# A two-dimensional spectral filter with FFN on one core: table loads, read back and the order of the spectral steps

## The chip, the cores and the metric

The kernel runs on one core of a Trainium2 chip. The metric is device time in microseconds for one execution of the whole program; the median of several runs counts. Engine names are those of the profile: PE (TensorE), PEld (its weight loads), DVE (VectorE), ACT (ScalarE), POOL (GpSimd), SP (SyncE).

## What is computed

The reference, cut to what matters, works on x of 2048 x 1024 in bf16:

```python
def A(x, w_r, w_i):                       # spectral filter
    X = rfft2(x.astype(f32))              # over both axes
    return irfft2(X * (w_r + 1j * w_i), s=(2048, 1024)).astype(bf16)
def B(x, w1, b1, w2):                     # FFN, 1024 -> 3584 -> 1024
    h = x @ w1 + b1
    return (h * tanh(softplus(h))) @ w2
x = x + A(layernorm(x)); x = x + B(layernorm(x))
x = x + A(layernorm(x)); x = x + B(layernorm(x))
```

So there are two spectral stages and two FFN stages, one after the other.

## The kernel before

The program is a list of instructions per engine (PE, DVE, ACT, POOL, SP) that a small planner in Python writes out. `Prog.add` puts down the waits: every tile has a `Res`, which knows its writers and readers, and each engine runs its list strictly in order. DMAs are issued from the lists of SP, POOL and ACT; an issue that has to wait stops everything behind it on that engine.

A spectral stage (`layer_A`) turns the two-dimensional transform into matmuls with tables. The 2048 rows are split into 16 x 128, the 1024 columns into 8 x 128. Stage 1 (`s1`, PE L635) transforms the short axes of both. Then the work is cut into eight groups, g = 0 to 7, of two slots each, and each group has four steps with two halves each:

- `s2(g, half)`, PE L741: the long column transform into Z. Half 0 is copied from PSUM by ACT (L776), half 1 by ACT or DVE (L776 or L778); the next step of either slot needs both halves.
- `s3(g, i)`, PE L786 to L789: the long row transform with the forward table FT, copied out by ACT (L793), then multiplied by the filter with four DVE instructions (L797 to L804), into YK.
- `i1(g, i)`, PE L815: the inverse row transform with the back table BT, copied into V by ACT (L826); group 7 is split between DVE and ACT (`copy`, L578 and L574).
- `i2(g, half)`, PE L840 and L872: the inverse column transform into U, copied by ACT (L884), or by DVE (L882) for (3, 1) and (5, 1); group 7 again split between both.

After the second half of `i2`, `u_turn` writes U to DRAM (`u_scratch`) and `u_back` reads an earlier group back with another layout into UT. Group 7 goes in two halves, both written from ACT's list, and `u_last` reads it in six parts, four from SP and two from ACT. When all of UT is there, the last short transform runs (`i4`, PE L1041). While PE waits for it, it runs `spin` (L652), `residual_first` (L1030) and `hold` (L657).

The order of the steps is written out by hand in `order_A`: "320" is step 3 (`s3`) of group 2, half 0; both spectral stages use the same list. Each step takes the next of four pairs of PSUM banks in turn (`pair`).

In the first spectral stage (li = 0) the filter of each group is made on the way: `filter_bins(g)` (PE L1002, two DVE copies L1013, two ACT copies L1017) follows s2(g, 1) for g = 0 and 1 and s2(g, 0) for the others; `load_w` brings its input over POOL's list, and `keep_filter` stores the result for the second stage, after s3(g, 1), from POOL's list too. In the second stage `load_w` reads the stored filter.

The tables FT and BT have rings of three slots. `open_tables` loads the first ones, from SP in the first stage and from POOL in the second (there already during the first FFN stage, since it is called from `layer_B`). The later ones are loaded from POOL, after s3(g, 1) for FT and i1(g, 1) for BT. All DMAs have line L251, that of the helper `dma`.

Of the kernel before, what the change touches and what calls it, by code (L numbers as in the profile page):

```python
# [180 lines left out]
class KB:  # L181
# [482 lines left out]
    def open_tables(self, li):  # L664

        self.li = li
        self.WT = self.ring("WT", 4 if li else 8, 2048, [2, 512])
        self.FTr = self.ring("FT", 3, 1536, [2, 384])
        self.BTr = self.ring("BT", 3, 1536, [2, 384])
        if li == 0:  # L670
            self.WR = self.ring("WR", 3, 4096, [2, 2, 512])
        for g in range(2):
            self.load_w(g)
        for g in range(2 + li):
            self.load_tabs(g, li == 0)
        for g in range(2):
            self.load_btabs(g, li == 0)

    def rest_of_filter(self):

        self.WT += [self.alloc(f"WT{i}", self.o["WT"] + 2048 * i, [2, 512]) for i in range(4, 8)]
        gate = Res("gate")
        for r in self.r_xr[1:3]:
            gate.inherit(r)
        for g in (2, 3):
            self.load_w(g, [gate])

    def load_tabs(self, g, sp=False):
        b = self.FTr[g % 3]
        self.dma(self.sp if sp else self.pool, b.ap, self.con["FT"][g], f"ft{g % 3}{sp}", writes=[b.res])  # L690

    def load_btabs(self, g, sp=False):
        b = self.BTr[g % 3]
        self.dma(self.sp if sp else self.pool, b.ap, self.con["BT"][g], f"bt{g % 3}{sp}", writes=[b.res])
# [9 lines left out]
    def load_w(self, g, after=()):  # L704
        if self.li == 0:
            self.load_wr(self.wr(g), g)
            return
        i = 2 * g % 8
        self.dma(self.pool, self.wt_pair(i), self.w_d[g], f"wt{g % 4}", reads=[self.r_wd[g]] + list(after), writes=[w.res for w in self.WT[i:i + 2]])

    def layer_A(self, li):
# [13 lines left out]
        def filter_bins(g):  # L725
            ps, banks, _ = self.pair()
            self.filter_bins(g, ps, banks, self.wr(g), WT[2 * g % 8:2 * g % 8 + 2], o["WT"] + 2048 * (2 * g % 8),
                             self.JT, self.r_jt, dve)

        def zslot(g, i):  # L730
            return Z[(2 * g + i) % 6]

        def s2(g, half):

            ps, banks, _ = self.pair()
            y = self.Y.ap
            at = lambda r: y[:, r * 8 + g, :]
            fns = []

            def mm(dst, r, t, n, start, stop):  # L740
                fns.append(lambda e: e.matmul(dst, at(r), FD[:, t:t + n], start=start, stop=stop))  # L741
            if half == 0:
                for i in range(2):
                    d = ps[:, i * 512:(i + 1) * 512].rearrange("p (r k) -> p r k", r=2)
                    for kd in range(2):
                        for c in range(2):
                            mm(d[:, :, kd * P:(kd + 1) * P], 4 * kd + 2 * c + i, kd * 512 + c * 256, 256, c == 0, c == 1)
            else:
                d3 = ps[:, 0:512].rearrange("p (s r k) -> p s r k", s=2, r=2)
                for i in range(2):  # L750
                    for c in range(2):
                        mm(d3[:, i, :, :], 8 + 4 * c + i, 1024 + c * 256, 256, c == 0, c == 1)

                dd = ps[:, 512:1024].rearrange("p (s r d k) -> p d s r k", s=2, r=2, d=2)
                for kd in range(2):
                    r, t = 10 + 4 * kd, (3 + kd) * 512
                    if g == 0:
                        for i in range(2):
                            mm(dd[:, kd, i, :, :], r + i, t, P, True, True)
                    else:  # L760
                        for c in range(2):
                            mm(dd[:, kd, :, :, :], r + c, t + c * 256, 256, c == 0, c == 1)
            self.group(fns, reads=[self.Y.res, self.r_fd], writes=banks)
            za, zb = zslot(g, 0), zslot(g, 1)

            zz = self.ARENA[:, o["Z"] // 2 + (2 * g % 6) * K:o["Z"] // 2 + (2 * g % 6 + 2) * K].rearrange(
                "p (s r k) -> p s r k", s=2, r=2)
            if half == 0:
                za.res.begin()
                zb.res.begin()  # L770
            dst, src = zz[:, :, :, 256 * half:256 * half + 256], ps.rearrange("p (s r k) -> p s r k", s=2, r=2)
            if half:
                dst = dst.rearrange("p s r (b k) -> p s r b k", b=2)
                src = ps.rearrange("p (b s r k) -> p s r b k", b=2, s=2, r=2)
            if half == 0 or g < 3:
                self.op(act, lambda e: e.activation(dst, src, ACT.Copy), reads=banks, parts=[za.res, zb.res])  # L776
            else:
                self.op(dve, lambda e: e.tensor_copy(dst, src), reads=banks, parts=[za.res, zb.res])  # L778
# [107 lines left out]
        def u_turn(g, half):  # L886

            u = U[g % 3]
            if g == 7:
                h = slice(8 * half, 8 * half + 8)  # L890
                if half == 0:
                    u_back(6)
                self.dma(act, self.u_d[g][:, h, :], u.ap[:, h, :], f"uwh{half}", reads=[u.res], writes=[self.r_ud7[half]])
                if half:
                    u_last()
            elif half:
                self.dma(sp, self.u_d[g], u.ap, f"uw{g % 3}", reads=[u.res], writes=[self.r_ud[g]])
                if g:
                    u_back(g - 1)

        def open_ut():
# [6 lines left out]
        def u_back(g):  # L908
            if self.UT is None:
                open_ut()  # L910
            self.dma(sp, self.UT.ap[g:P:8, :, :], self.u_d[g].rearrange("l r n -> r l n"), f"usp{g % 3}",
                     reads=[self.r_ud[g]], parts=self.r_ut)

        def u_last():

            def back(prog, half, q, n):
                l = slice(32 * q, 32 * q + 32 * n)
                self.dma(prog, self.UT.ap[7 + 64 * half:P if half else 64:8, l, :], self.u_d[7][l, 8 * half:8 * half + 8, :].rearrange("l r n -> r l n"),
                         f"ul{half}{q}", reads=[self.r_ud7[half]], parts=self.r_ut[q:q + n])
            back(sp, 0, 0, 2)  # L920
            back(sp, 0, 2, 2)
            for q in range(4):
                back((act, sp)[q % 2], 1, q, 1)
# [17 lines left out]
        for stage, g, h in self.order_A():  # L941
            if stage == 2:
                s2(g, h)
                if li == 0 and h == (g < 2):
                    filter_bins(g)
                    if g in (0, 1):
                        load_w(g + 5)
                    elif g == 4:
                        load_w(7)
            elif stage == 3:  # L950
                s3(g, h)
                if h:
                    if li <= g < 6:
                        load_tabs(g + 2)
                    if li == 0:
                        self.keep_filter(g)
                    elif g < 4:
                        load_w(g + 4)
            elif stage == 4:
                i1(g, h)  # L960
                if h and g < 6:
                    load_btabs(g + 2)
            else:
                i2(g, h)
                u_turn(g, h)
# [9 lines left out]
    @staticmethod  # L975
    def order_A():


        order = ("200 201 210 300 211 301 220 310 400 221 311 401 230 320 410 500 231 321 411 501 330 331 420 510 240 511 421 241 "
                 "250 251 340 341 520 350 430 260 521 431 440 261 351 441 530 531 360 361 450 451 540 541 550 270 551 271 460 461 "  # L980
                 "370 371 560 561 470 471 570 571")
        return [tuple(map(int, w)) for w in order.split()]

    def load_wr(self, wr, g):
# [798 lines left out]
```

## Time and profile before

| | |
|---|---|
| median of 6 runs | 930.54 us (927.76 to 933.35) |
| the profiled execution | 930.39 us, of it 928.5 us from the first to the last instruction (the span) |
| granted TensorE clock | 0.998 of full speed |
| PE busy | 879.3 us, 95% of the span |
| DVE, ACT, POOL busy | 67%, 47%, 17% |
| DMA | 175.99 MB, on average 190 GB/s |
| first spectral stage, groups | about 37 to 113 us |
| second spectral stage, groups | about 494 to 562 us |
| PE L1329 and L1230 (FFN) | 340.2 and 280.3 us busy |

How to read it: times on the timeline are microseconds from the start of the span. A line of the timeline has start, duration, engine, line of the kernel, operation and operands, the number of instructions merged into it, and in brackets the idle time of the engine before it with what ended that idle time. Ends of matmuls are modelled: on PE the distance from one start to the next says what a group of matmuls costs. The chain lists the work that ended last, followed back from the end, in order of time: start, duration, engine, line.

### The profile page before, as it was taken

The numbers are of one execution on the slowest core, as the hardware profiler recorded it, in microseconds if no ns is written. First come the engines' busy times: TensorE is split into PE (matmuls) and PEld (weight loads), VectorE is DVE, ScalarE is ACT, GpSimd is POOL, SyncE is SP. The second block draws the span as 40 slices with busy tenths as digits, with TensorE's granted clock in tenths as the row PEclk, the third lists the DMA queues.
The fourth block names the chain that finished last, engine by engine and source line by source line (L and its number), as shares of the span: only waits on it lengthen the run. The fifth ranks groups of instructions, "written<-read, shape, count | busy, mean of one in ns | idle before, by whom it ended". The sixth has DMA issues, their size and how long they took to land.

```text
span 928.5 us, 13616 instructions
## 1 busy us (share of the span) xinstructions
PE 879.3 (95%) x5503; PEld 471.2 (51%) x5503; DVE 620.2 (67%) x985; ACT 435.9 (47%) x645; POOL 159.0 (17%) x187
## 2 busy tenths in 40 slices
PE   0899889999999999999999988999999999999998
PEld 0667476444444444444456766754444444444443
DVE  7798368686789667568766755666747655554473
ACT  7998385456213485520019865757550015552000
POOL 5642003960004641010121200000000000000000
PEclk9999999999999999999999999999999999999999
DMA  9979762674786388364723894445156645832432
GB/s 295 286 226 280 205 187 63 222 277 123 277 258 244 141 314 295 127 228 143 283 91 114 227 223 129 152 159 169 50 191 192 194 134 193 277 120 84 172 121 111
DMA packets 145839, 175.99 MB, mean 190 GB/s; under 512 B 66904, under 2 KB 124344, under 8 KB 145656
## 3 DMA queue, kind: packets, MB, share of 16 engines
q1 hardware_dynamic: 132816, 128.29, 44.5%
q0 software_dynamic: 10864, 45.19, 13.6%
q10 hardware_dynamic: 2096, 1.64, 0.6%
q8 instruction: 43, 0.70, 0.3%
q14 instruction: 20, 0.16, 0.1%
HBM read 130.78 MB, written 40.89 MB: 185 GB/s over the span
## 4 chain that ended last, share of the span: by engine, by line
PE 86%; DMA 4%; DVE 4%; ACT 3%; SPq 2%; issue 1%; POOL 0%; ACTq 0%; DVEq 0%
PE PS L1329 35%; PE PS L1230 30%; PE PS L1190 6%; PE PS L741 3%; PE PS L815 3%; PE PS L840 2%; PE PS L1041 2%; SPq L251 2%; DMA ARENA<-in_A_x_dram 1%; DMA ARENA<-in_B_w_dram 1%; DMA u_scratch<-ARENA 1%; PE PS L1151 1%; DMA ARENA<-u_scratch 1%; ACT ARENA L452 1%; PE PS L786 1%; PE PS L652 1%
## 5 line engine op out<-in xcount | busy, mean ns | idle before, releaser
L1329 PE MATMUL PS<-ARENA 128*128 128x512 bf16 x1568 | 340.2, 379 | 0.2 <-DMA ARENA<-in_B_w_dram 0.2
L1230 PE MATMUL PS<-ARENA 128*128 128x512 bf16 (+1 forms) x1288 | 280.3, 379 | 0.8 <-DVE ARENA L1235 0.8
L1329 PEld LDWEIGHTS PS<-ARENA 128*128 128x128 bf16 x1568 | 153.3, 98 | 185.0 <-DVE ARENA L1372 0.7
L1235 DVE TENSOR_TENSOR ARENA<-PS,ARENA 128x512 f32<-128x512 f32 x230 | 157.0, 690 | 100.8 <-PE PS L1230 93.0
L1230 PEld LDWEIGHTS PS<-ARENA 128*128 128x128 bf16 x1288 | 125.4, 98 | 153.1 <-DVE ARENA L1235 3.5
L1240 ACT ACTIVATE ARENA<-ARENA,B 128x512 bf16<-128x512 f32 x138 | 98.8, 721 | 69.1 <-DVE ARENA L1235 63.8
L574 ACT ACTIVATE ARENA<-PS 128x512 f32<-128x512 f32 (+3 forms) x86 | 61.6, 726 | 113.9 <-PE PS L1230 92.9
L1123 POOL TENSOR_TENSOR ARENA<-ARENA 128x512 bf16<-128x512 bf16 x56 | 71.1, 1269 | 75.6 <-DVE ARENA L523 61.2
L452 ACT ACTIVATE ARENA<-XS 128x1024 bf16<-128x1024 bf16 x60 | 63.2, 1053 | 36.2 <-DVE XS L1380 33.0
L1190 PE MATMUL PS<-ARENA 128*128 128x256 bf16 (+1 forms) x528 | 75.0, 299 | 3.4 <-DVE ARENA L1156 1.9
L1354 DVE TENSOR_TENSOR ARENA<-ARENA 128x3584 bf16<-128x3584 bf16 x32 | 63.8, 2015 | 0.0
L1190 PEld LDWEIGHTS PS<-ARENA 128*128 128x128 bf16 x528 | 50.9, 99 | 23.0 <-DVE ARENA L1156 3.3
L1380 DVE TENSOR_TENSOR XS<-PS,ARENA 128x512 bf16<-128x512 f32 x52 | 35.7, 689 | 38.9 <-PE PS L1329 38.5
L1372 DVE TENSOR_TENSOR ARENA<-PS,ARENA 128x512 f32<-128x512 f32 x48 | 32.9, 687 | 28.0 <-PE PS L1329 27.6
L1194 ACT ACTIVATE ARENA<-PS,B 128x256 bf16<-128x256 f32 (+1 forms) x66 | 33.2, 515 | 30.3 <-PE PS L1190 30.0
L1240 ACT ACTIVATE ARENA<-PS,B 128x512 bf16<-128x512 f32 x46 | 31.5, 685 | 18.4 <-PE PS L1230 18.4
L1368 DVE TENSOR_TENSOR ARENA<-ARENA,XS 128x512 f32<-128x512 f32 x52 | 36.8, 731 | 0.6
L443 ACT ACTIVATE RS<-MV,EPS 128x1 f32<-128x1 f32 (+2 forms) x11 | 3.3, 296 | 71.7 <-DVE MV L565 70.1
L797 DVE TENSOR_TENSOR ARENA<-ARENA 128x1024 bf16<-128x1024 bf16 x32 | 22.0, 687 | 20.5 <-ACT ARENA L793 14.8
L815 PE MATMUL PS<-ARENA 128*128 128x256 bf16 x256 | 32.3, 273 | 3.3 <-DVE ARENA L804 3.2
L793 ACT ACTIVATE ARENA<-PS 128x1024 bf16<-128x1024 f32 x32 | 32.7, 1052 | 4.8 <-PE PS L789 4.8
L741 PE MATMUL PS<-FD,ARENA 128*128 128x256 bf16 (+1 forms) x256 | 31.8, 271 | 2.5 <-ACT ARENA L641 1.3
(100 smaller groups left out, 823.8 us busy)
## 6 DMA issues: line engine op xcount, KB each, us to landing
ARENA<-in_B_w_dram SPq DMA_DIRECT2D x30, 896.0 KB, 6.8
ARENA<-w1s_scratch SPq DMA_DIRECT2D x28, 896.0 KB, 4.7
ARENA<-w2s_scratch SPq DMA_DIRECT2D x24, 896.0 KB, 6.6
w1s_scratch<-ARENA POOLq DMA_DIRECT2D x14, 896.0 KB, 4.4
ARENA<-in_B_w_dram SPq DMA_DIRECT2D x24, 512.0 KB, 4.3
u_scratch<-ARENA SPq DMA_DIRECT2D x14, 512.0 KB, 3.9
ARENA<-u_scratch SPq DMA_DIRECT2D x14, 512.0 KB, 6.8
w2s_scratch<-ARENA POOLq DMA_DIRECT2D x8, 896.0 KB, 4.1
```

Source lines behind the costliest of these rows:

```text
L452: self.op(act, lambda e, i=i, f=f: e.activation(junk.ap, x, f, accum_out=sums[:, i:i + 1]), reads=[self.r_xs[j]], writes=[junk.res], parts ...
L574: fn = (lambda e: e.activation(dst, src, ACT.Copy)) if scale is None else \
L741: fns.append(lambda e: e.matmul(dst, at(r), FD[:, t:t + n], start=start, stop=stop))
L815: fns.append(lambda e, c=c, part=part: e.matmul(ps[:, c * 256:(c + 1) * 256], yk.ap[:, part, c * P:(c + 1) * P], t[:, (128, 0)[part]:(384, ...
L1123: self.op(self.pool, lambda e, dst=A(dst), x=A(x), y=A(y), op=op: e.tensor_tensor(dst, x, y, op), reads=[b.res] + list(after), writes=[b.rs])
L1190: fns.append(lambda e, db=db, bank=bank, fl=fl: e.matmul(PS[:, bank, 0:w], wb.ap[:, db, fl * P:(fl + 1) * P], x.ap[:, db, tok], start=(db ...
L1230: self.group([lambda e, db=db: e.matmul(PS[:, bank, :], A[:, db, :], mov[:, db, :], start=(start and db == 0), stop=(db == 3), skip_group_ ...
L1235: self.op(dve, lambda e: e.tensor_tensor(dst.ap, PS[:, bank, :], x.ap, ALU.add), reads=[self.r_bank[bank], x.res], writes=[dst.res])
L1240: self.op(act, lambda e: e.activation(at, src, ACT.Mish, bias=self.B1[:, ft:ft + 1]), reads=[res, self.r_b1], writes=[ra])
L1329: self.group([lambda e, i=i, k=k, b=PB[n][k].ap: e.matmul(PS[:, bank, :], ap[:, i, t * P:(t + 1) * P], b[:, i - 7 * k, :], start=(start an ...
L1354: self.op(dve, lambda e: e.tensor_tensor(ap[dst][:, f, :], ap[x][:, f, :], ap[y][:, f, :], op), reads=part(x, k) + part(y, k), writes=part ...
L1368: self.op(dve, lambda e: e.tensor_tensor(a[t], a[t], x, ALU.add), reads=[rx], writes=[r[t]])
```

## The change

Five edits, all in the spectral stage:

- Forward table 2 is loaded in `open_tables` in both stages, after the back tables. In the first stage this moves it from POOL's list, where it stood after s3(0, 1), to SP's; in the second it stays with POOL, now behind the two back tables instead of ahead of them.
- The copy of s2(1, 1) goes from ACT to DVE.
- `u_back(5)` stands ahead of the write of group 6 on SP, not behind it.
- 211 comes before 300 in the order (with it filter 1, in the first stage).
- At the end of the order 270 and 271 come before 450 to 551 (270 and filter 7 before 450, 271 before 540), and 370 comes before 461.

```diff
@@ open_tables
-        for g in range(2 + li):
+        for g in range(2):
             self.load_tabs(g, li == 0)
         for g in range(2):
             self.load_btabs(g, li == 0)
+        self.load_tabs(2, li == 0)
@@ s2
-            if half == 0 or g < 3:
+            if half == 0 or g in (0, 2):
                 self.op(act, lambda e: e.activation(dst, src, ACT.Copy), reads=banks, parts=[za.res, zb.res])
             else:
                 self.op(dve, lambda e: e.tensor_copy(dst, src), reads=banks, parts=[za.res, zb.res])
@@ u_turn
             elif half:
+                if g == 6:
+                    u_back(5)
                 self.dma(sp, self.u_d[g], u.ap, f"uw{g % 3}", reads=[u.res], writes=[self.r_ud[g]])
-                if g:
+                if 0 < g < 6:
                     u_back(g - 1)
@@ layer_A, after s3(g, 1)
-                    if li <= g < 6:
+                    if 1 <= g < 6:
                         load_tabs(g + 2)
@@ order_A
-        order = ("200 201 210 300 211 301 220 310 400 221 311 401 230 320 410 500 231 321 411 501 330 331 420 510 240 511 421 241 "
-                 "250 251 340 341 520 350 430 260 521 431 440 261 351 441 530 531 360 361 450 451 540 541 550 270 551 271 460 461 "
-                 "370 371 560 561 470 471 570 571")
+        order = ("200 201 210 211 300 301 220 310 400 221 311 401 230 320 410 500 231 321 411 501 330 331 420 510 240 511 421 241 "
+                 "250 251 340 341 520 350 430 260 521 431 440 261 351 441 530 531 360 361 270 450 451 271 540 541 550 551 460 370 "
+                 "461 371 560 561 470 471 570 571")
```

## The prediction

> **What bounds the kernel now.** I read the page first, then the PE waits, the chain in the two spectral stages, and the timelines of PE, ACT, DVE and SP there. The span is 928.5 us and PE is busy for 95% of it at a granted clock of 0.998, so only PE's gaps can be won. The change touches the spectral stage alone, which runs twice: stage one from about 37 to 113 us, stage two from 494 to 562. In these, three gaps matter. The first is in stage one:
>
> ```profile
> 49.36 1.04 PE L741 MATMUL PS<-FD,ARENA 128*128 128x256 bf16 x8
> 50.23 0.62 PE L1002 MATMUL PS<-ARENA 128*128 128x256 bf16 x4
> 52.61 0.38 PE L786 MATMUL PS<-ARENA 128*128 128x512 bf16 x1 [1.76 <-DMA ARENA<-c_ft]
> ```
>
> Step 320 (stage 3, group 2, half 0) waits for forward table 2, which POOL issued at 48.16 and which took 4.3 us to land. Group 3's filter ends at 50.23 + 0.46 = 50.69, so the gap is 1.9 us from start to start. The second gap is the chain at the end of the stage:
>
> ```profile
> 92.31 1.94 ACT ARENA L826 x2
> 94.25 0.93 ACT ARENA L793
> ...
> 95.27 0.69 DVE ARENA L797
> ...
> 99.41 1.06 PE PS L815 x8
> ...
> 104.08 5.13 DMA u_scratch<-ARENA
> ...
> 109.23 3.77 DMA ARENA<-u_scratch
> ```
>
> Two ACT copies of group 6's V, then the copy of 370, then eight DVE instructions (two halves of 2.0 us), and only then 471; after it copies, 57x, the write of group 7's second half and its read back, for which the final transform (L1041) waits at 113.24. Stage two has the same shape with a shorter write:
>
> ```profile
> 555.05 3.13 DMA u_scratch<-ARENA
> 558.20 3.88 DMA ARENA<-u_scratch
> ```
>
> Elsewhere in the stages PE runs back to back, and after them it mostly does; all later loads follow engine progress, so I pass a shift at the end of a stage on to the end of the run one for one. Between these gaps DVE is nearly as full as PE; this matters now.
>
> **Part 1: table 2 by SP, and 211 ahead of 300, stage one.** Table 2 leaves POOL's queue (issue 1.38 us) and becomes one more SP issue after the back tables, near 36.3 us. The two SP tables took 6.3 us each, so it lands near 42.6, over 7 us early; the small loads behind it move by about 0.8 us (BD landed at 43.0, first used at 54.3: covered). POOL's later tables move forward too, since group 1's filter releases its load sooner. So the 1.9 us goes, and I ask what is late next. Durations from rows, as one instruction follows the next: PE 0.87 per step (filter 0.46), ACT 0.905 per copy (filter 0.74), DVE 2.0 per half of stage 3, 1.3 per filter, 1.2 per PSUM copy.
> - Copy 211 moves from ACT to DVE. DVE was idle for 4.33 us before 43.02, so copy 211 (41.25 to 42.4) and filter 1 (to 43.8) fit there, but half 300 now starts at 43.8 instead of 43.02.
> - DVE is then solid: five halves, filters 2 and 3 (300, 301, F2, 310, 311, F3, 320) end at 43.8 + 5 x 2.0 + 2 x 1.3 = 56.4; before it was 56.94. Copy 231 ends at 57.6 (before 58.16).
> - PE would reach 330 at 56.8: 400 waits for DVE until 45.86 (45.63 before), then 0.87 or 0.46 each with no gap. But 330 reads what copy 231 writes, so it starts at 57.7. Before, it started at 58.69.
> So the gap of 1.9 us gives **0.99 us**; DVE takes back the rest. Ends: 0.6 if a copy of PSUM runs late, 1.9 if 330 did not wait.
>
> **The same in stage two.** There table 2 was loaded at 396.7 to 399.4, a hundred us before use; putting it behind the back tables costs nothing. Only 211 ahead of 300 counts. PE waits 0.50 us before 300 at 496.76 for ACT's copy of 201; 211 fills that (496.10 to 496.97) and goes 0.21 over. The chain 300, ACT 793, DVE's four instructions ended at 501.04, just when PE came to 400 at 501.11. It is now 0.21 later, and PE, earlier by 0.66, waits for it. Result: **0.2 us lost**; ends 0.3 lost, 0 with DVE's start unchanged.
>
> **Part 2: the last steps in another order, both stages.** 270 and 271 (and in stage one filter 7) go ahead of 450 to 551, and 370 ahead of 461. The work PE does before 470 is the same. ACT: 460 copied at 92.31 to 93.2, then 370 instead of 461, done at 94.1 instead of 95.05. DVE has done filter 7 and copies 271 and 551 by 92.6, so 370's half runs from 94.3 to 96.3 and 371's to 98.3 (before 99.36; ACT's copy of 371 at 96.0 hides in 370's half). Step 470 has its data when PE arrives at 97.1 (560 waits 0.4 for 461's copy, covered by the wait that follows); 471 starts about **0.95 us** earlier, and all behind it. Stage two's rows give the same 0.95 (370's half starts at 545.28 instead of 546.25). Ends: 0.5, 1.1.
>
> So the second half of group 7 is issued by ACT at 104.08 - 0.99 - 0.95 = 102.14, and in stage two at 555.05 + 0.2 - 0.95 = 554.3.
>
> **Part 3: read back 5 ahead of write 6.** Reading back 5 waits for write 5 to land, and write 6 is now queued behind that wait on SP; behind write 6 stand read 6 and four of the six last reads. In the new order copy 551 comes about 1 us later against the step behind it, so write 5 is issued near 91.6 (91.72 before) and 543.9 (542.76). It took 7.3 and 5.2 us. So SP is free for write 6 between 96.8 and 98.9 (stage one, 97.94 before) and near 549.1 (548.99). The read goes sooner, the write does not: I take read 6 to land where it did, at 107.6 and 557.1 to 558. The queues' work is the same; what is won is that two idle us of the DMA engines (548 to 550) are filled, and that filter 7's store, issued at 91.44, goes about 3 us earlier.
>
> What the last write costs is bounded by its own rows: first and second half took 4.4 and 5.1 in stage one, 3.6 and 3.1 in stage two. The second half now stands to read 6 as the first half did (about 1 us and 1.9 us behind it), so I take 4.4 and 3.6. Landing: 106.54 (109.21 before) and 557.9 (558.18). Gains: **2.67 and 0.3 us**. PE is not the limit: it waited 1.25 and 0.31 us before L1041 at the end of filler matmuls that move along with it, which caps stage one's gain at 1.94 + 1.25 = 3.2.
>
> [...]
>
> **Sum.** Stage one 2.67, stage two 0.3: 2.97 us off the profiled execution's 930.39 (span 928.5 and 1.89 around it) gives 927.4; the median shown is 930.54, 0.15 more, so I say **927.5**. The ends: stage one 1.1 (0.6 + 0.5, no gain in landing) to 3.9 (1.9 + 1.1, landing shortened until PE caps it); stage two from a loss of 1.8 (0.3 - 0.5, and the write at 5.1 instead of 3.1) to a gain of 1.1. Together from 0.7 lost to 5.0 won.
>
> **Rivals.**
> - *All of it is won.* If DVE is not what 330 waits for (its instructions overlap by up to 0.1 us each, and 231's copy may slip in) the table's 1.9 us comes whole, and with less in the queues the writes take 3.1. Stage one 3.9, stage two 0.75: 925.7. For it: PE has no other listed wait between 52 and 97. Against: DVE's solid run from 43 to 60.
> - *The gaps change names.* 330 waits for DVE, 471 comes early, but read 5, read 6 and the last write meet in the queues and land as late as before, but for a little. 1 us in all: 929.5. For it: the DMA engines are at 9 tenths or more nearly throughout 93 to 107 us.
> - *Slower: write 6 is held up by the read that was put ahead of it.* Place: SP, after 551. If write 5 takes 7.3 us in both stages and write 6 then takes what write 5 took (7.3, 5.2), read 6 is issued at 106.5 and 556.8 and lands 5.6 or more later, 112.1 and 562.4, with the last SP reads behind it, near 114.4 and 564.6 against 113.24 and 562.21: 3.5 us lost, 934.0. It decides from the point where read 6 lands later than about 110 and 559, the times at which the last reads are under way now. Against it: DMA engines had idle slices at 88, 91 and 548, and in stage two write 5 had 5.2 with the same neighbours.
>
> **Chances.** Forecast 0.49, all won 0.26, names changed 0.15, slower 0.10. A measurement of this kernel can tell about 0.3% (2.8 us) from no change. The forecast lies close to that bound: two thirds of it count as faster, one third as the same. All won is faster, names changed is the same, and of the slower case 0.07 is beyond the bound and 0.03 within. So faster 0.59, same 0.34, slower 0.07. The range holds the forecast's ends and the two neighbours: 925.0 to 931.0; above it lies the slower case.
>
> **What would show it.** In the new profile the wait for the table at L786 is gone, and a wait of about 0.9 us for DVE L778 stands before 330 near 57. In stage two 400 waits about 0.9 us for DVE L804. The wait of 470 is gone and 471 waits 0.3 to 0.8 us. ACT issues the last write 2 us after the start of read 6 or sooner, it takes 3.6 to 4.4 us, and L1041 starts near 110.6 and 561.9. I am wrong if 330 follows 501 without a gap, if write 6 is issued more than 1 us later than before, or if the last write takes over 5 us.

## The result and the profile after

The median went from 931.08 us (927.75 to 935.83, 65 runs) to **927.48 us** (925.38 to 931.91, 30 runs): a ratio of 0.9963, 95% interval 0.9953 to 0.9972, which is 3.45 us off (2.6 to 4.4); the two medians lie 3.60 apart. The forecast was 927.5. The profiled execution of after took 928.0 us: a span of 926.2 at a granted clock of 1.000.

Below, "at +x" is a time counted from the first s2 matmul of the stage it belongs to, since that start itself moves between executions: in stage one it lay between 36.6 and 39.3 us over the profiles of this case. The two profiled executions, cut into stretches (us):

| stretch | before | after | difference |
|---|---|---|---|
| start to first s2, stage one | 37.31 | 38.55 | +1.24 |
| s2 to last transform, stage one | 75.93 | 73.71 | -2.22 |
| to first s2 of stage two | 380.46 | 380.70 | +0.24 |
| s2 to last transform, stage two | 68.51 | 68.56 | +0.05 |
| from there to the end | 366.33 | 364.66 | -1.67 |

The stretches that the change edits gave 2.17, all of it in stage one; the prediction had 2.97, with 0.3 in stage two. Another 1.67 came from a stretch that no edit touches. First the steps that went as predicted. The timeline of PE in stage one of after:

```profile
57.84 0.40 PE L873 MATMUL PS<-ARENA,BD 64*128 64x128 bf16 x8
58.91 0.39 PE L787 MATMUL PS<-ARENA 128*128 128x512 bf16 x1 [0.68 <-DVE ARENA L779]
```

and of DVE beside it:

```profile
57.30 0.42 DVE L805 TENSOR_TENSOR ARENA<-ARENA 128x512 bf16<-128x512 bf16 x1
57.64 1.22 DVE L779 CAST ARENA<-PS 128x1024 bf16<-128x1024 f32 x1
```

The wait for the table at L787 (L786 of before) is gone. In its place 330 waits for copy 231, which DVE starts only when the half of 320 is through, at 57.64. 330 starts at +20.36 instead of +21.38. The chain at the end of stage one in after (start, duration, engine, line):

```profile
92.73 1.02 ACT ARENA L827
93.76 0.92 ACT ARENA L794
...
94.70 0.69 DVE ARENA L798
...
98.85 1.06 PE PS L816 x8
...
103.52 4.39 DMA u_scratch<-ARENA
...
107.93 4.09 DMA ARENA<-u_scratch
```

One copy of V stands ahead of 370's copy, not two, the DVE work follows at once, and the last write takes 4.39 us instead of 5.13. The chain of stage two in after:

```profile
551.79 0.61 ACT ARENA L574
...
552.48 2.82 DMA u_scratch<-ARENA
555.30 0.02 issue
555.32 5.96 DMA ARENA<-u_scratch
```

Here the chain has changed: it no longer goes through the second half's write (issued 553.54, landed 555.92), but through the first half's and then 5.96 us of reading. Those reads were issued on SP behind read 6 (554.69). The list of SP shows why they are late; before:

```profile
548.99 0.32 SPq L251 DMA_DIRECT2D u_scratch<-ARENA  x1
549.36 11.07 SPq L251 DMA_DIRECT2D ARENA<-u_scratch  x6
```

and after:

```profile
545.63 3.77 SPq L251 DMA_DIRECT2D ARENA<-u_scratch  x2
549.44 1.44 SPq L251 DMA_DIRECT2D u_scratch<-ARENA  x1
554.69 5.44 SPq L251 DMA_DIRECT2D ARENA<-u_scratch  x5
```

Stage two began 0.74 us earlier in after, so its write 6, issued at 549.44, is 1.2 later by the stage's own time (+56.48 against +55.29). About half of this is the copy of 561 that it writes out, which ends at +55.82 instead of +55.27; the rest is read 5, which stands ahead of it on SP and goes out at 548.86, when write 5 has landed (548.84). Write 6 then took 5.2 us beside read 5, which now runs with it, against 3.1 before, and read 6 could only be issued when it had landed, at 554.69 (+61.7, before +58.4). Read 6 landed at 559.7, by the stage's own time 3.3 later than before: 1.2 from the late issue of write 6 and 2.1 from its longer time. The last write landed 1.5 us sooner than before, and that was worth nothing.

That the read ahead of it lengthens write 6 shows in all fourteen profiles: in stage two write 6 took 3.1 to 3.5 us in the seven kernels with read 5 behind it, and 4.1 to 5.5 in the seven with read 5 ahead.

**The stretch that no edit touches** is shorter by the granted clock. Windows of 2 us after stage two's last transform in before (columns: window, length, busy time of PE, PEld, DVE, ACT and POOL, granted clock, DMA share, GB/s):

```profile
566.00:568.00 2.00, 1.26 (x28) 1.08 (x26) 1.85 (x6) 1.57 (x3) 0.00 (x0) 1.00 1.06 315
568.00:570.00 2.00, 1.12 (x23) 0.97 (x19) 1.37 (x4) 2.00 (x4) 0.00 (x0) 1.00 1.17 307
570.00:572.00 2.00, 1.07 (x9) 0.69 (x7) 2.00 (x4) 1.98 (x3) 0.00 (x0) 0.83 1.11 281
572.00:574.00 2.00, 2.00 (x12) 1.37 (x10) 1.90 (x6) 1.34 (x3) 0.00 (x0) 0.50 0.25 70
574.00:576.00 2.00, 2.00 (x26) 1.79 (x25) 1.72 (x10) 1.07 (x2) 0.00 (x0) 0.81 0.00 0
```

and of the same place in after:

```profile
566.00:568.00 2.00, 1.09 (x20) 0.91 (x20) 1.53 (x6) 1.60 (x5) 0.00 (x0) 1.00 1.18 309
568.00:570.00 2.00, 1.07 (x16) 0.90 (x16) 1.74 (x4) 2.00 (x4) 0.00 (x0) 1.00 1.19 297
570.00:572.00 2.00, 1.55 (x15) 1.40 (x16) 1.97 (x5) 1.97 (x3) 0.00 (x0) 1.00 0.97 237
572.00:574.00 2.00, 2.00 (x30) 1.87 (x28) 1.83 (x7) 1.88 (x4) 0.00 (x0) 1.00 0.04 12
```

The instructions and the waits ahead of them are the same; in before the clock then goes to half, and 16 matmuls (L1190, in after L1193) take 3.44 us, against 1.92 in after, which is 1.52 of the 1.67 us. The timeline of PE, before and then after:

```profile
571.14 3.44 PE L1190 MATMUL PS<-ARENA 128*128 128x256 bf16 x16 [0.93 <-DVE ARENA L1156]
570.45 1.92 PE L1193 MATMUL PS<-ARENA 128*128 128x256 bf16 x16 [0.93 <-DVE ARENA L1159]
```

The prediction read the 0.998 of before on the page and made nothing of it.

### The profile page after: what moved, and what is told of

Same layout as the page of the kernel before. It is cut to its first block, busy times and chain, and to the rows that moved or that the text cites. A ratio compares the mean times of both kernels' runs of the same rounds, so it can differ in the third digit from the quotient of the medians.

```text
span 926.2 us, 13613 instructions
## 1 busy us (share of the span) xinstructions
PE 878.7 (95%) x5503; PEld 471.8 (51%) x5503; DVE 622.4 (67%) x987; ACT 434.9 (47%) x643; POOL 157.8 (17%) x186
## 4 chain that ended last, share of the span: by engine, by line
PE 85%; DVE 6%; DMA 3%; ACT 3%; SPq 2%; issue 1%; ACTq 0%; DVEq 0%
PE PS L1332 37%; PE PS L1233 30%; PE PS L1193 6%; PE PS L742 3%; PE PS L816 2%; PE PS L841 2%; SPq L251 2%; PE PS L1044 2%; DMA ARENA<-in_A_x_dram 1%; DMA ARENA<-u_scratch 1%; PE PS L1154 1%; DMA u_scratch<-ARENA 1%; PE PS L635 1%; ACT ARENA L452 1%; DVE ARENA L798 1%; DVE ARENA L800 1%
## 5 line engine op out<-in xcount | busy, mean ns | idle before, releaser
L574 ACT ACTIVATE ARENA<-PS 128x512 f32<-128x512 f32 (+3 forms) x86 | 61.7, 727 | 110.9 <-PE PS L1233 92.7
L1193 PE MATMUL PS<-ARENA 128*128 128x256 bf16 (+1 forms) x528 | 73.4, 295 | 3.4 <-DVE ARENA L1159 1.9
L1193 PEld LDWEIGHTS PS<-ARENA 128*128 128x128 bf16 x528 | 50.2, 98 | 22.3 <-DVE ARENA L1159 3.3
L1208 DVE TENSOR_TENSOR ARENA<-ARENA 128x2048 f16<-128x2048 bf16 x16 | 25.4, 1587 | 9.0 <-PE PS L1193 8.7
```

The source lines that it names most:

```text
L574: fn = (lambda e: e.activation(dst, src, ACT.Copy)) if scale is None else \
L1193: fns.append(lambda e, db=db, bank=bank, fl=fl: e.matmul(PS[:, bank, 0:w], wb.ap[:, db, fl * P:(fl + 1) * P], x.ap[:, db, tok], start=(db ...
```

## The experiments

The times are medians; the ratio, with its 95% interval, is to runs of before taken beside them. There were four such batches: runs 1 to 4, 5 to 8, 9 and 10, 11 and 12. The median of before in them was 931.03, 931.57, 931.02 and 931.63 us. Behind each ratio stands what the trace shows, in "at +x".

**1. The table load alone**, on before (`open_tables`, and the condition of the later loads):

```diff
-        for g in range(2 + li):
+        for g in range(2):
...
+        self.load_tabs(2, li == 0)
...
-                    if li <= g < 6:
+                    if 1 <= g < 6:
```

> Only the load of table 2 is changed (SP, after the back tables). Offsets are counted from a stage's first s2 matmul; before, 330 starts at 21.38 us and L1041 at 75.93 in stage one, 400 at 7.41 and L1041 at 68.51 in stage two. Theory (DVE is the next wait): DVE runs without a gap from half 300 to the copy of 231 whether PE stalls or not, so 330 can gain only what it had in hand after that copy, 0.4 us: 330 at about 20.9, L1041 0.4 sooner, the whole kernel 0.4 us faster at most. Rival (the table was the whole gap): 330 at 19.5 and 1.9 us in all. Stage two unchanged in both.

928.35 us, 0.9972 [0.9953, 0.9991]. The timeline of PE:

```profile
56.10 0.40 PE L873 MATMUL PS<-ARENA,BD 64*128 64x128 bf16 x8
57.45 0.39 PE L787 MATMUL PS<-ARENA 128*128 128x512 bf16 x1 [0.95 <-DVE ARENA L779]
```

330 at +20.89: 0.49 of the 1.76 us of table wait is kept, DVE takes the rest. So the rival that all of it is won falls. Yet stage one is 0.80 shorter in the profile, and the measured time 2.7 us: more was won than the trace of one execution of before had to give.

**2. The start alone**: the table load as in run 1, copy 211 on DVE and 211 ahead of 300, on before.

```diff
-            if half == 0 or g < 3:
+            if half == 0 or g in (0, 2):
...
-        order = ("200 201 210 300 211 301 220 310 400 221 311 401 230 320 410 500 231 321 411 501 330 331 420 510 240 511 421 241 "
+        order = ("200 201 210 211 300 301 220 310 400 221 311 401 230 320 410 500 231 321 411 501 330 331 420 510 240 511 421 241 "
```

> Table 2 by SP, 211 ahead of 300 and its copy on DVE; the end of the order and the reads as before. Theory: 330 at 20.4, with a wait of 0.7 us for the copy of 231 before it; L1041 of stage one 1.0 us sooner (74.9); in stage two 400 at 7.54 instead of 7.41 and L1041 0.1 later (68.6). In all 0.9 us. Rival (the first steps' order is worth nothing beside the table): 330 as in the kernel with the table alone.

928.84 us, 0.9964 [0.9945, 0.9983]. 330 at about +20.4, as in after: moving 211 adds 0.5 to the table load. The last transforms start at +74.27 and +68.94. Part 1 by itself has, within the intervals, the whole measured gain of the change, where 0.9 us was expected of it.

**3. The tail alone**: only the end of the order, on before.

```diff
-                 "250 251 340 341 520 350 430 260 521 431 440 261 351 441 530 531 360 361 450 451 540 541 550 270 551 271 460 461 "
-                 "370 371 560 561 470 471 570 571")
+                 "250 251 340 341 520 350 430 260 521 431 440 261 351 441 530 531 360 361 270 450 451 271 540 541 550 551 460 370 "
+                 "461 371 560 561 470 471 570 571")
```

> Only the end of the order is changed. Theory (the late read 6 of stage two comes from the write of group 6 standing behind read 5 on SP): with the old reads, 471 starts 0.8 to 0.95 us sooner in both stages and the last write and reads follow: L1041 at about 74.5 in stage one and 67.7 in stage two, 2 us in all. Rival (writes 4 and 5 come later in the new order, and that alone fills the queues): 471 is as much sooner, but L1041 of stage two stays near 68.5, about 1.2 us in all.

932.23 us, 1.0012 [0.9994, 1.003]. In stage two the residual matmuls start 0.9 earlier (+61.32 against +62.23), and the last transform 1.07 later (+69.58). Write 5 is issued at +49.94 instead of +49.06, and what stands behind it is late with it: read 6 goes out 0.6 later (+58.95) and then takes 6.9 us instead of 5.0. Stage one says little here, for it was hit twice by the clock, at the first s2 matmuls (16 in 3.15 us, in before 1.69) and behind the table wait; the timeline of PE there:

```profile
52.87 0.62 PE L1002 MATMUL PS<-ARENA 128*128 128x256 bf16 x4
55.75 0.59 PE L786 MATMUL PS<-ARENA 128*128 128x512 bf16 x1 [2.26 <-ACT ARENA L1017]
...
57.41 1.90 PE L815 MATMUL PS<-ARENA 128*128 128x256 bf16 x8
```

The table wait is there again, longer (POOL issued the load at 50.80, 4.8 us before it landed; the releaser named is an ACT copy that had long been done), and the eight matmuls after it take 1.90 us, not 1.05. The windows show it:

```profile
54.00:56.00 2.00, 0.25 (x1) 0.14 (x2) 1.97 (x6) 2.00 (x4) 1.93 (x4) 0.94 0.99 294
56.00:58.00 2.00, 2.00 (x7) 0.90 (x6) 1.64 (x4) 0.46 (x2) 0.00 (x0) 0.50 0.99 343
58.00:60.00 2.00, 2.00 (x15) 1.55 (x13) 1.29 (x2) 1.33 (x2) 0.00 (x0) 0.71 0.97 390
```

**4. The read alone**: only `u_back(5)` ahead of write 6, on before.

```diff
             elif half:
+                if g == 6:
+                    u_back(5)
                 self.dma(sp, self.u_d[g], u.ap, f"uw{g % 3}", reads=[u.res], writes=[self.r_ud[g]])
-                if g:
+                if 0 < g < 6:
```

> Only read back 5 goes ahead of the write of group 6. Theory: SP holds write 6 until write 5 has landed, and write 6 then runs beside a read: write 6 is issued 1 us or more later in stage one (write 5 landed at 99.0), read 6 lands later in both, L1041 0.5 to 1 us later in stage one (76.4 to 76.9) and 0 to 1 later in stage two. In all 0.5 to 2 us slower. Rival (idle time of the queues is filled, and the last reads come sooner): L1041 0.3 to 0.8 sooner in both, about 1 us faster.

933.19 us, 1.0018 [0.9991, 1.0044]. In stage two nothing moves on PE until the residual matmuls (+62.24, as before); the last transform comes 1.26 later (+69.77). Write 6 goes out on time there (+55.30) but takes 4.6 us instead of 3.1. By itself this part of the change costs time in the trace of stage two; the medians can't tell it from before. Stage one began at half clock (the first 16 s2 matmuls took 3.15 us, in before 1.69), so its trace says little.

**5. After once more**, as a yardstick for single profiles.

> The changed kernel a second time, for the spread of a profile and for the count of stretches at half clock. If the profile shown is typical: 330 at 20.4 us after the first s2 matmul, L1041 at 73.7 in stage one and 68.6 in stage two, mean granted clock 0.998 to 1.0, 3.5 us faster than before. If its stage two was a lucky one (tail and read, each alone, had 69.6 and 69.8): L1041 at 69.5 or later there.

928.7 us, 0.9971 [0.9952, 0.999]. The last transform of stage two at +68.24 (+68.56 in the first profile). A stretch at half clock from 37.0 to 40.4 us lengthened the first steps of stage one, so that 330 comes at +21.88.

**6. After with the old read**: only write 6 ahead of read 5 again.

```diff
-                if g == 6:
-                    u_back(5)
...
-                if 0 < g < 6:
+                if g:
```

> The changed kernel with read 5 behind write 6 again. Theory (read 5 ahead costs as much as it brings): stage one and two within 0.5 us of the changed kernel, 73.7 and 68.6, time the same within 0.1%. Rival 1 (the late writes 4 and 5 of the new order are what hurts, and read 5 ahead mends it): L1041 of stage two at 69.6, as with the tail alone, 1 us slower than the changed kernel. Rival 2 (read 5 ahead holds write 6 and hurts): L1041 of stage two near 67.8, 0.8 us faster than the changed kernel.

928.38 us, 0.998 [0.9963, 0.9996]. The last transform of stage two at +69.05, 0.5 and 0.8 later than in the two profiles of after. With the new tail the read helps in these traces; the medians (928.38, and 928.7 in run 5) don't show it.

**7. After with copy 231 on ACT**, stage one only.

```diff
-            if half == 0 or g in (0, 2):
+            if half == 0 or g in (0, 2) or (g == 3 and li == 0):
```

> The changed kernel with the copy of 231 on ACT in stage one. Theory (330 waits for DVE's copy, and DVE has no slack there): the wait of 0.7 us before 330 is gone, 330 at 19.7 us after the first s2 matmul instead of 20.4, L1041 of stage one up to 0.7 sooner (73.0), 0.3 to 0.7 us faster than the changed kernel. Rival (ACT is as full and gives it back by the copies behind it): 330 at 19.7, but spin and L1041 as in the changed kernel.

928.29 us, 0.9972 [0.9956, 0.9988]. 330 starts at +19.52 with no wait, 0.84 sooner: the copy on DVE was what it waited for. But 0.54 of it is gone by the residual matmuls (46.01 us after 330, in after 45.47), and the time is that of after.

**8. Before with the table wait filled**: eight filler matmuls in stage one just ahead of 320, into PSUM banks that 320 then overwrites. Nothing of the computation is left out.

```diff
         for stage, g, h in self.order_A():
+            if li == 0 and (stage, g, h) == (3, 2, 0):
+                self.spin(8, 2 * (self.npair % 4))
```

> The kernel before with eight filler matmuls (1.7 us, 128x512, result overwritten) ahead of 320 in stage one, so that PE does not idle while table 2 is on its way. Theory (a wait of 2 us there costs more than itself: where the tail alone waited 2.26 us, PE then ran at half clock for 3.5 us): no stretch at half clock near 54 to 60, the mean clock of the runs rises and the kernel is 0.5 to 1 us faster than before, though the table still comes as late. Rival (the stretches at half clock belong to the start and to the end of stage two): no change, or 0.2 slower by the filler that outlasts the wait.

930.09 us, 0.9996 [0.9979, 1.0014]. The wait ahead of 320 is 0.25 instead of 1.76 and the stage no shorter, as meant. The time can't be told from before's. The granted clock can: 10 of 12 runs had a mean clock of 1.000, of before 12 of 34 in the same batch.

**9 and 10. Late tail**: after, but with 270 and 271 behind 450 to 550, so that 540 to 551 and the writes behind them stand where they did; 370 stays ahead of 461. Once with the new read, once with the old.

```diff
-                 "250 251 340 341 520 350 430 260 521 431 440 261 351 441 530 531 360 361 270 450 451 271 540 541 550 551 460 370 "
+                 "250 251 340 341 520 350 430 260 521 431 440 261 351 441 530 531 360 361 450 451 540 541 550 270 271 551 460 370 "
```

> The changed kernel with 270 and 271 left behind 550, so that only 271 goes ahead of 551 and 370 ahead of 461 (540 and 541, and so write 4, stay at their old place). Theory (the 0.8 to 0.9 us at 471 come from 370 ahead of 461 alone; what the queues take back in stage two comes from writes 4 and 5 being pushed behind 270 and 271): from 330 to the residual matmuls 45.5 and 43.5 us as in the changed kernel (before: 46.3 and 44.4), and from there to L1041 in stage two 6.1 to 6.5 instead of the changed kernel's 6.6 to 7.1; L1041 of stage two at 67.6 to 68.0, 0.3 to 0.7 us faster than the changed kernel in all. Rival (the late write 5, or read 5 ahead of write 6, is what lengthens it): 6.8 or more as in the changed kernel.

> The same with read 5 behind write 6, as before the change. Theory (with write 4 on time, the read's place matters little): from the residual matmuls to L1041 in stage two 6.1 to 6.5 us, L1041 at 67.6 to 68.0. Rival (read 5 ahead is needed as soon as write 5 is late): 7.5 or more, as with the tail alone (8.3) and with the changed kernel and the old read (7.6).

927.62 us, 0.9959 [0.9941, 0.9977], and 928.12 us, 0.9974 [0.9956, 0.9992]. The residual matmuls of stage two start at +61.46 in both, as in after (+61.45): the tail's gain on PE is kept without 270 and 271 ahead of 450 to 550. From there to the last transform of stage two it takes 6.92 and 6.99 us. With the old read, writes on time save 0.6 (7.59 in run 6); with the new one nothing (7.11 and 6.78 in after). So the late writes look like a cause with the old read only, but 0.6 us between single profiles is less than their spread (see below).

**11. Read 6 on POOL**: after, with read 6 issued from POOL's list, so that the last reads do not stand behind it on SP.

```diff
-                    u_back(6)
+                    u_back(6, pool)
```

> The changed kernel with read 6 issued from POOL instead of SP; everything else as changed. Theory (stage two now ends by write 6, read 6 and the last SP reads, which stand behind read 6's packets in the same queue; the last write no longer sets the end): the last SP reads land 4 us after they are issued instead of 6, from the residual matmuls to L1041 5.8 to 6.3 us in stage two instead of 6.6 to 7.1, L1041 at 67.3 to 67.8; 0.5 to 1 us faster than the changed kernel. Rival (read 6 itself lands last, or the DMA engines are simply full): 6.6 or more, no change, and a slower issue on POOL may make it 0.5 us slower.

931.46 us, 1.0008 [0.9994, 1.0022]. The issue took 1.07 us at 556.77 and the read landed 7.0 us after it, at 563.8. The chain of stage two:

```profile
555.33 2.26 DMA u_scratch<-ARENA
557.59 0.02 issue
557.61 6.64 DMA ARENA<-u_scratch
```

The theory that the last reads only wait in line behind read 6 falls: with read 6 out of SP's queue they take 6.64 us, not less than the 5.96 of after, and they end 0.45 us after read 6. PE waits 2.38 and 2.21 us before the two last transforms (0.83 and 1.14 in after). Why the reads are slower is not shown.

**12. All three that had helped or might**: read 6 on POOL, late tail, copy 231 on ACT.

> The changed kernel with three edits together: read 6 from POOL, 270 and 271 left behind 550, and the copy of 231 on ACT in stage one. If the theories hold: 330 at 19.5 us, L1041 at 73.0 to 73.5 in stage one and 67.3 to 67.8 in stage two, 1 to 1.5 us faster than the changed kernel, about 925.8 to 926.5 where that has 927.5. Rival (each gain is taken back by the next wait): within 0.5 us of the changed kernel.

928.25 us, 0.9971 [0.9956, 0.9986]. No better than after. None of the twelve beats after by more than the intervals.

## Why the prediction was right, and where it was not

**Right: the table and DVE.** "So the gap of 1.9 us gives 0.99 us; DVE takes back the rest." 1.02 came, with 0.68 of wait for the copy of 231 at 330; run 1 (half the gain without 211's move) and run 7 (no wait with the copy on ACT) show that DVE takes the rest. Half 300 starts on DVE at 45.05, +6.50; the forecast, 43.8, is +6.49. On the way there filter 2 waits 0.46 us for ACT, which the forecast had not; it cost nothing, since 330 waits for DVE.

**Right: the loss in stage two.** 400 waits 0.64 us for DVE L805 (forecast about 0.9) and starts at +7.54 instead of +7.41: 0.13 lost, forecast 0.2. The line in after:

```profile
500.50 1.05 PE L816 MATMUL PS<-ARENA 128*128 128x256 bf16 x8 [0.64 <-DVE ARENA L805]
```

**Right: the tail on PE.** From 330 to the residual matmuls it took 45.47 us instead of 46.26 in stage one and 43.46 instead of 44.38 in stage two: 0.79 and 0.92, forecast 0.95. 471 waits 0.19 us (forecast 0.3 to 0.8).

**Right in stage one, and there by luck: the last write.** It took 4.39 us in stage one (forecast 4.4), but not for the reason given. The forecast let it run about 1 us behind read 6, as the first half had; it went out 0.8 us ahead of read 6 (103.52 against 104.28), and the first half now took 2.45. In stage two it took 2.4, where 3.6 was said.

**Failed: "I take read 6 to land where it did, at 107.6 and 557.1 to 558."** Two steps ahead of it failed. The first: "SP is free for write 6 ... near 549.1 (548.99)". In stage two write 6 went out 1.2 us later by the stage's own time, which is one of the prediction's own signs of being wrong (more than 1 us). The second is a term that the sum leaves at nothing: write 6 was to take no longer with read 5 beside it, and took 5.2 us instead of 3.1. So read 6 landed 3.3 later, with the last reads behind it: the last transform starts 5.6 us after the last write has landed, not 4.0. In stage one write 6 went out on time (+60.55, before +60.63) and took 5.2 us instead of 4.2; read 6 landed 1.2 later (at 110.1), and the last reads took 0.3 longer. So the tail's 0.92 us in stage two reached PE and went no further. This is the slower rival's mechanism, in stage two past the point from which it was to decide (559 at before's times; 559.7 is 560.4 there). It cost less than the 3.5 us named, for write 5 took 5.5 and 5.8 us in the two stages, not the 7.3 that the rival reckoned with.

How the two parts play together shows in the time from the residual matmuls to the last transform of stage two, in us, one entry for each profile (runs 11 and 12, with read 6 on POOL, left out):

| | old read | new read |
|---|---|---|
| old tail | 6.28, 5.81, 6.56, 5.81 | 7.54 |
| new tail | 8.26, 7.59 | 7.11, 6.78, 6.62 |
| late tail | 6.99 | 6.92 |

Each part alone adds 1.4 us or more to this time; with the new tail the read takes about 1.1 back (means 7.9 and 6.8), which leaves 0.7 more than before (6.1). That eats most of the 0.8 by which the residual matmuls come earlier (+61.45 instead of +62.23). Two profiles with the same code in this place differ by up to 0.8, so single cells carry no more than that.

The sum lets the last write land ahead of a read 6 that is issued before it (106.54 against 107.6 in stage one). After is no test of that, since read 6 was issued behind the last write there (104.28 against 103.52, and 554.69 against 553.54), but other traces show such landings. In run 9, stage two, the last write was issued at 552.95, behind read 6 (552.29), and landed at 556.26, 1.4 us ahead of it (557.66); in run 4, stage one, it landed 0.6 us ahead (111.53 and 112.09). In before the first half of group 7 in stage one landed at 107.38, ahead of read 6 (107.67), which was issued 0.9 us earlier.

**The total was right by luck, through a second error.** The stages gave 2.17 us against 2.97. What made up for it lay in no term of the sum. The table wait is not it: with the old load and no filler it was 1.76, 2.26 and 1.42 us (before, runs 3 and 4), so the one that I read was no short one. That 320 started at +16.98 and +16.16 in runs 3 and 4, not at +15.30, comes mostly from the first 16 s2 matmuls, which took 3.15 us there at half clock and 1.69 in before. What did differ is the clock. Each profile's stretches at half clock are 3.41 us long (the one at the very end of the program left out), and each lowers the mean clock of a run by about 0.002. Runs of before at 0.998 took 1.7 to 2.6 us longer than those at 1.000, by batch. So the stretches can be counted without a trace:

| | runs at 1.000 | mean of those, us | mean of all, us |
|---|---|---|---|
| before, four batches | 38 of 113 | 929.1 to 929.8 | 931.2 to 931.4 |
| after, its own batch | 11 of 30 | 926.6 | 927.7 |
| after once more (batch 2) | 8 of 11 | 928.4 | 928.5 |
| table alone (batch 1) | 6 of 12 | 927.6 | 929.1 |
| start alone (batch 1) | 9 of 12 | 928.3 | 928.6 |
| tail alone, read alone (batch 1) | 0 of 12, 0 of 12 | | 932.4, 933.5 |
| after with old read (batch 2) | 2 of 12 | 927.3 | 928.9 |
| after with 231 on ACT (batch 2) | 4 of 12 | 927.9 | 928.6 |
| before, table wait filled (batch 2) | 10 of 12 | 930.0 | 930.7 |
| late tail, new and old read (batch 3) | 5 of 10, 5 of 11 | 926.7, 927.8 | 927.6, 928.8 |
| read 6 on POOL (batch 4) | 0 of 12 | | 932.1 |
| all three (batch 4) | 4 of 12 | 926.9 | 928.2 |

In batch 2 the means differ by 2.84 us between before (931.33) and after once more (928.49), among runs at 1.000 by 1.43 (929.81 and 928.38): about half of the gain lies in the mixture of clocks. For the result itself the share is smaller. After's own batch has 11 of 30 at 1.000, hardly more than before elsewhere; by the mean clocks (0.9985, before 0.9977 to 0.9980 in the four batches) the clock is worth an estimated 0.5 to 0.8 us of the 3.45. What is left holds the stages' 2.17 within the interval. In the other batches the share is less sure: start alone won 2.8 on all runs and 0.8 on those at 1.000.

Whether the change makes the stretches rarer is not shown: the same kernel, after, had 11 of 30 runs at 1.000 and 8 of 11. The fill of run 8 (10 of 12 runs at 1.000, before beside it 12 of 34) points to the table wait as one cause, and so does tail alone, where a stretch begins with the matmuls that follow that wait (2.26 us). But of the 14 stretches in the 14 profiles that is the only one; four begin with the first s2 matmuls of stage one, and nine 0.6 to 10 us after a last transform has started, as before's own at 571.34. In the 3.41 us ahead of that one PE was busy for 1.61 (47%) and no wait was over 0.93 us. What decides whether a stretch falls stays open: waits of 2.29 us (tail alone) and 2.21 us (read 6 on POOL) before stage two's last transform had none behind them. Open too is how much of run 1's gain is wait and how much is clock.

## What to carry to other kernels

A read that waits and is put ahead of a write on a queue that is issued in order can cost twice: the write may go out later (here by nothing to 0.9 us, with the same tail), and it then runs beside the read (4.1 to 5.5 us instead of 3.1 to 3.5). Work out when the last transfer behind it lands, not when the first one goes. When a wait is removed, follow the next engine by its solid run of instructions; its end gave the gain here to 0.03 us, where the length of the wait was nearly twice too much. And before a gain is summed from one execution, look whether that execution holds a stretch at a lower clock or a wait that varies between runs: here, in one batch, about half of the gain lay in the clock.

## What was not expected of the hardware

- In before the granted clock was half for 3.41 us from 571.34; in the 3.41 us ahead of that PE was 47% busy and no wait was above 0.93 us. In after, with the same instructions and waits at that place, it stayed at 1.00.
- A write of 512 KB to DRAM that took 3.1 us in stage two of before took 5.2 in after beside a read of the same size that was issued 0.6 us ahead of it.
- A write issued from ACT 0.7 us behind a read issued from SP landed 1.4 us ahead of it (run 9, stage two).
- The same read issued from POOL took 1.07 us to issue and landed 7.0 us after the start of its issue in run 11 and 5.8 in run 12; from SP it had taken 5.0.
